# Batch 7 by block products too, with sums and softmax steps merged, and one pool of output tiles

## The chip, the core and the metric

The kernel runs on one core of a Trainium2 chip. The time is the device time of one execution in microseconds (us). TensorE (PE in the views; its weight loads are PEld) multiplies matrices into PSUM, which has eight banks of 512 fp32 columns here; VectorE (DVE) and ScalarE (ACT) read PSUM and SBUF; GpSimd (POOL) works from SBUF to SBUF and issues the loads; SyncE (SP) issues most stores. Each engine takes its instructions in order and waits on semaphores.

## What is computed

From the reference, for each of 8 batches b and 8 heads (576 tokens s, head size 64, 32 memory slots m):

```
a = exp(phi - max(phi));  a = a / sum(a)                 # over the 32 slots
k_m = a^T k;   v_m = a^T v                               # 32 x 64 per head
attn = softmax(scale * q @ k_m^T) @ v_m
x = attn, heads side by side                             # 4608 tokens x 512
h = max(x @ w1, x @ w2, x @ w3)                          # 4608 x 768
out = h @ w_out                                          # 4608 x 512, float32
```

## The kernel before

One function lays down every instruction; the order of the whole program is a list of words written out by hand at its end (manual schedule, line 55; the loop that reads the words ends the function). A word is a step, an index, "@" and a batch: `A1@3` is step A, index 1, batch 3 (batch 9 means the weights common to all batches). A "!" swaps the engine that a step uses by default. `issue` (L726) maps words to functions. An engine executes its instructions in the order of this list, each as soon as what it needs is there, so a step can run well before an earlier word of another engine. The PSUM banks that the steps take are a string of digits read off in the same order (L142).

The steps, by batch:

- Loads, all issued by POOL: L0 phi, L1 k, L2 v, L3 q (L85 to L112); r copies k beside v (L102; POOL, or ACT with "!").
- E: exp of phi (ACT). B: k_m and v_m (PE, L255). N: normalise (DVE). K: transposes (PE, L305) and their copy out of PSUM (L176 is the ACT branch of the common `evacuate`, L180 the DVE branch).
- Q0, Q1: q transposed in 32x32 blocks (DVE, L320). S: scores (PE, L340) and their exp (ACT, L349). Then the softmax over 32 slots, for each of two groups of heads by itself: a (DVE transpose, L394), s (DVE sum, L402), c (DVE reciprocal, L411), m (multiply, POOL L416, DVE with "!"), X (DVE transpose back, L424). Batch 0 and half of batch 1 do it another way (M, R, X with `ones_mul`).
- D0 to D3: v_m folded into the weights (PE L447, copied by ACT or DVE). So the product with the values needs only the softmax weights `attn` (256 rows) as input; V (DVE, L217, sources in SBUF) replaces w1 and w2 by their differences from w3, and the third term comes back as `wp3`, the fold of w3 times w_out.
- F0 to F11: the hidden layer, transposed (PE L473, four matmuls of 288 columns). Even steps write `h` (relu, ACT L174; DVE L178 with "!"); odd ones take the maximum with it into `hT` (DVE L486, one source in PSUM, one in SBUF).
- T0 to T4: an output tile of 128 tokens (PE, L662 six matmuls of hT and w_out, L671 two of attn and wp3, 512 columns each), copied by ACT or DVE and stored by SP. T4 is the tile of 128 tokens that spans the end of one batch and the start of the next; its attn part goes in two halves of 64 (L680). The last tile of all, T3@7, goes in two column halves (`ffn2_last`, L694: L703, L711) so that half is copied and stored while the other is computed.
- For batches 2 to 6 the 512 tokens outside T4 go by seven block products instead of eight (Strassen's scheme in Winograd's form): tokens, hidden rows and output columns are each cut in two. U0 to U3 form the sums of weight blocks (for batch 9 of w_out, for the others of wp3), A0 to A3 those of hT and A4 to A7 those of attn (`combine`, L509 to L511: POOL; DVE for U with "!" and for A without). P0 to P6 are the products (`products`, L569; PE L604: eight matmuls of 256 columns each), some of which add up in one bank, with copies taken of it in between (`snap`, `ln`, L618 or L616); sums and copies go into two fixed tiles `oj` (L645, L618, L616) that SP stores by block rows, 512 KB each (L649).

Batches 0, 1 and 7 go by token tiles: T0 to T3. `sums` (L525) puts the A sums of hT into space of w3 that is free by then, those of attn into `sa0`; hT and attn of two batches lie in two tiles.

Of the kernel before, what the change touches and what calls it, by code (L numbers as in the profile page):

```python
# [15 lines left out]
def kernel(  # L16
# [92 lines left out]
    def load_q(b):  # L109
        qq = inp.tile([P, NP, NC, D], BF16, name="qq", tag="qq")  # L110
        loaded.setdefault(b, {})["q"] = qq
        nc.gpsimd.dma_start(  # L112
            out=qq.rearrange("p j c d -> p j (c d)"), in_=by_pair(q, b)
        )
# [22 lines left out]
    for i in range(P // M):  # L137
# [7 lines left out]
            00232204420145545045024602460260426042672640640460246206420402640246240760260420  # L145
            64026402640264070462064026304620464060460624062403620460642640266042046204264260
            5620566620520652046262042062606262042640240630101323
# [177 lines left out]
    attns = {}  # L325

    def att_score(b):
# [4 lines left out]
        if b // 2 not in attns:  # L332
            attns[b // 2] = work.tile([P, NG, 2 * S], BF16, name="attn")
# [56 lines left out]

    def att_t(b, g):
        s = st[b]
        t = s["t", g] = work.tile([P, S // HP, R, 2], BF16, name="t", tag=f"t{g}")
        nc.vector.transpose(  # L394
            out=t.rearrange("p n r e -> p (n r e)").bitcast(FP32),
            in_=s["e2"][:, g].bitcast(FP32),
        )

    def att_sum(b, g):
        s = st[b]  # L400
        sm = s["sm", g] = work.tile([P, S // HP, 2], FP32, name="sm", tag=f"sm{g}")
        nc.vector.tensor_reduce(  # L402
            out=sm,
            in_=s["t", g].rearrange("p n r e -> p n e r"),
            op=ALU.add,
            axis=mybir.AxisListType.X,
        )

    def att_rec(b, g):
        s = st[b]  # L410
        nc.vector.reciprocal(out=s["sm", g], in_=s["sm", g])  # L411

    def att_mul(b, g, swap):
        s = st[b]
        t = s["t", g]
        (nc.vector if swap else nc.gpsimd).tensor_tensor(  # L416
            out=t,
            in0=t,
            in1=s["sm", g].unsqueeze(2).to_broadcast([P, S // HP, R, 2]),
            op=ALU.mult,  # L420
        )

    def att_back(b, g):
        nc.vector.transpose(  # L424
            out=attns[b // 2][:, g, (b % 2) * S : (b % 2 + 1) * S].bitcast(FP32),
            in_=st[b]["t", g].rearrange("p n r e -> p (n r e)").bitcast(FP32),
        )
# [32 lines left out]
    hts = {}  # L460
    fts = {}

    def ffn1(b, n, swap):
        s = st[b]
        ft, w = n // 2, n % 2
        if b // 2 not in hts:
            hts[b // 2] = work.tile([P, FT, 2 * S], BF16, name="hT")
# [16 lines left out]
        else:  # L484
            fts.setdefault(b, []).append(ft)
            nc.vector.tensor_tensor(  # L486
                out=hT[:, ft, (b % 2) * S : (b % 2 + 1) * S].rearrange("p (h n) -> p h n", h=2),
# [15 lines left out]
    sa0 = const.tile([P, 4, TW], BF16, name="sa0")  # L503
    oj0 = [const.tile([P, 2, DM], FP32, name=f"oj{i}") for i in range(2)]
# [20 lines left out]
    def sums(b):  # L525

        if b not in sas:
            if b == B - 1:
                s = inp.tile([P, NP, NC, D], BF16, name="sx", tag="qq")
                s = s.rearrange("p j c d -> p (j c d)").rearrange("p (i n) -> p i n", i=3)  # L530
                sa = inp.tile([P, NP, NC, D], BF16, name="sy", tag="qq")
                sa = sa.rearrange("p j c d -> p (j c d)")[:, 0 : 4 * TW]
                sa = sa.rearrange("p (i n) -> p i n", i=4)
            else:
                s, sa = w_sb[:, 0:3, 2], sa0
            sas[b] = (
                s.rearrange("p i (k q n) -> p i k q n", k=KT, q=2),
                sa.rearrange("p i (q n) -> p i q n", q=2),
            )
        return sas[b]  # L540

    def blocks(x, b, k):

        c0 = (b % 2) * (S + HP)
        x = x[:, :, c0 : c0 + 2 * TW]
        return [
            [
                x[:, k * i : k * (i + 1)].rearrange("p f (q r n) -> p f q r n", q=2, r=2)[
                    :, :, :, r
                ]  # L550
                for i in range(2)
            ]
            for r in range(2)
        ]

    def combine_a(b, i, on_dve):

        s, sa = sums(b)
        n = i % 4
        if i < 4:  # L560
            (a11, a12), (a21, a22) = blocks(hts[b // 2], b, KT)
            t = {0: s[:, 0], 1: s[:, 1], 2: a21, 3: s[:, 2]}
        else:
            (a11, a12), (a21, a22) = blocks(attns[b // 2], b, 1)
            t = {m: sa[:, m : m + 1] for m in range(4)}
        in0, in1 = [(a21, a22), (t[0], a11), (a11, a21), (a12, t[1])][n]
        combine(on_dve, t[n], in0, in1, ADD if n == 0 else SUB)

    def products(b, i, swap):  # L569

        s, sa = sums(b)
        h, a = blocks(hts[b // 2], b, KT), blocks(attns[b // 2], b, 1)
        wp3 = wp3s[b]

        def plain(r, c):
            return lambda k, q: h[r][c][:, k, q] if k < KT else a[r][c][:, 0, q]

        def summed(n):
            src = h[1][0] if n == 2 else s[:, min(n, 2)]
            return lambda k, q: src[:, k, q] if k < KT else sa[:, n, q]  # L580
# [43 lines left out]
        if "ot" not in acc:  # L624
            if b == B - 1:
                ot = [inp.tile([P, NP, NC, M], FP32, name=f"ox{n}", tag="ph") for n in range(2)]
                acc["ot"] = [
                    x.rearrange("p j c m -> p (j c m)")[:, 0 : 2 * DM].rearrange(
                        "p (q n) -> p q n", q=2
                    )  # L630
                    for x in ot
                ]
            else:
                acc["ot"] = oj0
        acc[i] = True
        done = [2] if i == 2 else [i] if i > 4 else [4] if 3 in acc and 4 in acc else []
        for n in done:
            ot = acc["ot"][n // 5][:, :, slice(0, CH) if n in (2, 6) else slice(CH, DM)]
# [7 lines left out]
            if n in (4, 6):  # L646
                r0 = b * S + (b % 2) * HP
                rows = out[r0 : r0 + 2 * TW].rearrange("(q r p) c -> p q r c", q=2, r=2)
                nc.sync.dma_start(out=rows[:, :, n // 5], in_=acc["ot"][n // 5])  # L649
# [3 lines left out]
    def ffn2(b, t, swap):  # L653
# [4 lines left out]
        if b == B - 1 and t == 3:  # L658
            return ffn2_last(b, c0)
        po = one_bank()  # L660
        for n, fc in enumerate(fts[b]):
            nc.tensor.matmul(  # L662
                po,
                lhsT=hT[:, fc, c0 : c0 + P],
# [23 lines left out]
        ot = opool.tile([P, DM], FP32, name="ot")  # L688
# [5 lines left out]
    def ffn2_last(b, c0):  # L694

        hT, attn = hts[b // 2], attns[b // 2]
        ot = opool.tile([P, DM], FP32, name="ot")
        r0 = (b // 2) * 2 * S + c0
        for i in range(2):
            c = slice(i * DM // 2, (i + 1) * DM // 2)  # L700
            po = one_bank()[:, 0 : DM // 2]
            for n, fc in enumerate(fts[b]):
                nc.tensor.matmul(  # L703
                    po,
                    lhsT=hT[:, fc, c0 : c0 + P],
                    rhs=wo_sb[:, fc, c],
                    start=(n == 0),
                    stop=False,
                )
            for g in range(NG):  # L710
                nc.tensor.matmul(  # L711
                    po,
                    lhsT=attn[:, g, c0 : c0 + P],
                    rhs=wp3s[b][:, g, c],
                    start=False,
                    stop=(g == NG - 1),
# [9 lines left out]
    def issue(b, n, swap):  # L726
# [6 lines left out]
            "L": lambda: load_ph(b) if i == 0 else load_q(b) if i == 3 else load_kv(b, i - 1),  # L733
            "H": lambda: load_kv(b, i % 2, halves[i // 2]),
# [27 lines left out]
    for w in """  # L762
# [3 lines left out]
        D2@0 D4@0 F4@0 L0@1 V1@0 F1@0 E@1 F3@0 L1@1 F5@0 F9@0 F7@0 L3@1 F11@0 L2@1 B0@1  # L766
        T2@0! N0@1 Q1@1 K0@1 L0@2 Q0@1 T1@0 S@1 U0@9 B1@1 U1@9 M1@1 U3@9! V2@0 N1@1 L1@2
        L2@2 K1@1! R1@1 L0@3 L3@2 a0@1 D0@1 L1@3 s0@1 D1@1! T0@0! r0@2 c0@1 m0@1! X0@1
        D2@1 X1@1 F6@1! F0@1 F10@1! F4@1! F1@1 F11@1 E@2 F8@1 F2@1 L2@3 F5@1 B@2 D3@1
        N@2 F3@1 L3@3 F7@1 K@2! F9@1 D3@2 L1@4 D0@2 L0@4 T3@0 Q1@2 U0@2 Q0@2 D2@2! S@2  # L770
        U1@2 a0@2 E@3 r0@3! s0@2 L2@4 L3@4 U2@9 c0@2 T3@1 T0@1! a1@2 m0@2 T4@1! D1@2!
        B@3 s1@2 c1@2 X0@2 m1@2 X1@2 F0@2 N@3 U3@2 Q0@3 A4@2! F6@2 A5@2! F1@2 U2@2 F8@2
        Q1@3 F2@2 L1@5 F7@2 L0@5 K@3! F4@2 F3@2 S@3 L2@5 A6@2! F5@2 A7@2! F10@2 a0@3
        D2@3 D0@3 D3@3 L3@5 a1@3 r0@4 s1@3 E@4 c1@3 s0@3 m1@3 c0@3 T1@1 F9@2 m0@3 F11@2
        T2@1! X0@3 D1@3! B@4 X1@3 N@4 F4@3 F6@3! F0@3 A0@2! F10@3 Q0@4 U0@3 Q1@4 A1@2!
        F8@3 F5@3 K@4! F9@3 U1@3 P1@2! S@4 A2@2! a0@4 A3@2! s0@4 D1@4! c0@4 L1@6 P0@2
        F11@3 P2@2 a1@4 s1@4 E@5 F7@3 P4@2 F2@3 c1@4 r0@5! F3@3 P5@2! F1@3 U3@3 L0@6
# [47 lines left out]
```

## Time and profile before

| | us |
|---|---|
| median of 3 runs (lowest, highest) | 163.0 (162.53, 163.24) |
| the profiled execution, whole | 162.93 |
| its span, first to last instruction | 161.2 |
| mean granted clock of TensorE | 0.997 |
| busy PE, DVE, ACT, POOL | 150.9, 113.0, 101.8, 103.8 |

The profile is of one execution. Its page gives the busy time of each engine, digits for 40 equal slices of the span, the chain of work that ended last, and the costliest groups of instructions (line, engine, operation, shapes, count; busy time and mean ns of one; idle time before them and what ended it). Other views of the same trace used below: the chain of waits in order of time, the timeline of a stretch, the table of stretches (busy time of each engine, granted clock, DMA share), and the DMA issues with the time from issue to landing.

### The profile page before, as it was taken

To read this page: it belongs to the slowest core of one execution; us is meant where nothing else is said; L and a number is where in the kernel's file an instruction comes from. 1 tells how busy PE (TensorE), PEld (TensorE's weight loads), DVE (VectorE), ACT (ScalarE), POOL (GpSimd) and SP (SyncE) were. 2 spreads that over 40 slices of the span, in tenths; PEclk is the share of its full clock that TensorE was granted. 3 is DMA by queue.
4 is the path that set the end of the run, shared out by engine and by line. 5 is a ranking of instruction groups with operands and counts; after the bars stand their busy time and mean duration, and the time that the engine had idled before them with its cause. 6 is when DMAs were issued, how large, how long until landed. Compare 5 with 4: busy or idle time off the path is not lost.

```text
span 161.2 us, 5135 instructions
## 1 busy us (share of the span) xinstructions
PE 150.9 (94%) x2190; PEld 98.5 (61%) x2202; DVE 113.0 (70%) x216; ACT 101.8 (63%) x144; POOL 103.8 (64%) x118
## 2 busy tenths in 40 slices
PE   7988698999899999899999999999999999999991
PEld 2343444673467346556788774887775878885660
DVE  2022702999878896697989799899889669785330
ACT  3205335943895798698598999977859864423110
POOL 7932135641056499979997999989959995840000
PEclk9999999999999999999999999999999999999998
DMA  5999999999999999999999999999304300601463
GB/s 154 188 204 191 194 210 212 279 207 276 251 277 259 208 228 229 338 225 223 317 213 240 211 331 230 176 230 268 133 32 168 132 4 0 260 0 40 162 255 133
DMA packets 21814, 31.78 MB, mean 197 GB/s; under 512 B 1056, under 2 KB 16416, under 8 KB 21792
## 3 DMA queue, kind: packets, MB, share of 16 engines
q0 software_dynamic: 16080, 21.43, 70.4%
q1 hardware_dynamic: 5568, 9.90, 17.2%
q8 instruction: 17, 0.28, 0.6%
q10 hardware_dynamic: 144, 0.13, 0.2%
q14 instruction: 5, 0.04, 0.1%
HBM read 39.32 MB, written 9.44 MB: 303 GB/s over the span
## 4 chain that ended last, share of the span: by engine, by line
PE 82%; DMA 9%; POOL 2%; ACT 2%; issue 2%; DVE 1%; ACTq 0%; DVEq 0%; POOLq 0%
PE psum L473 30%; PE psum L604 19%; PE psum L662 12%; DMA wo_sb<-in_moe_w_out_dram 9%; PE psum L447 5%; PE psum L196 3%; PE psum L671 3%; PE psum L255 3%; PE psum L340 2%; PE psum L680 1%; PE psum L305 1%; PE psum L703 1%; POOL ko L97 1%; ACT e L349 1%; DVE h L178 0%
## 5 line engine op out<-in xcount | busy, mean ns | idle before, releaser
L473 PE MATMUL psum<-attn,wp 128*128 128x288 bf16 x384 | 52.5, 286 | 0.2
L473 PEld LDWEIGHTS <-wp 128*128 128x128 bf16 x384 | 36.7, 98 | 11.0 <-issue 1.5
L486 DVE TENSOR_TENSOR hT<-psum,h 128x576 bf16<-128x576 f32 x48 | 34.5, 745 | 4.9 <-PE psum L473 3.2
L176 ACT CAST wp<-psum 128x1024 bf16<-128x1024 f32 (+1 forms) x30 | 28.4, 993 | 4.1 <-PE psum L447 2.8
L174 ACT ACTIVATE h<-psum 128x576 bf16<-128x576 f32 x36 | 22.3, 658 | 6.4 <-PE psum L473 6.2
L662 PE MATMUL psum<-wo_sb,hT 128*128 128x512 bf16 x81 | 21.0, 380 | 0.6 <-issue 0.2
L176 ACT COPY ot<-psum 128x512 f32<-128x512 f32 x14 | 8.1, 591 | 14.9 <-PE psum L671 8.1
L416 POOL TENSOR_TENSOR t<-t,sm 128x576 bf16<-128x576 bf16 x12 | 13.7, 1157 | 3.6 <-DVE sm L411 3.6
L662 PEld LDWEIGHTS <-hT 128*128 128x128 bf16 x90 | 8.2, 98 | 9.7 <-issue 1.7
L163 PE MATMUL psum<-warm 128*128 128x512 bf16 x42 | 12.5, 455 | 1.4 <-DVE warm L130 1.2
L604 PEld LDWEIGHTS <-hT 128*128 128x128 bf16 x120 | 11.5, 98 | 2.7 <-issue 0.9
L349 ACT ACTIVATE e<-psum 128x576 bf16<-128x576 f32 x16 | 9.5, 650 | 5.2 <-PE psum L340 5.1
L320 DVE STREAM_TRANSPOSE qT<-qq 128x576 f32<-128x576 f32 x16 | 11.7, 758 | 0.9 <-DMA qq<-in_q_dram 0.8
L178 DVE TENSOR_SCALAR h<-psum 128x576 bf16<-128x576 f32 x12 | 8.9, 752 | 3.5 <-PE psum L473 2.9
L511 POOL TENSOR_TENSOR w_sb<-hT 128x768 bf16<-128x768 bf16 x5 | 8.2, 1643 | 4.1 <-DVE hT L486 4.1
L233 ACT ACTIVATE e<-ph 128x1152 bf16<-128x1152 f32 (+1 forms) x9 | 9.7, 1073 | 1.9 <-DMA ph<-in_phi_dram 1.8
L645 DVE TENSOR_TENSOR oj<-psum,snap 128x512 f32<-128x512 f32 x10 | 6.8, 683 | 5.6 <-PE psum L604 3.9
L107 POOL COPY kvr<-ko 128x2304 bf16<-128x2304 bf16 x2 | 4.2, 2116 | 9.2 <-DMA ko<-in_k_dram 9.2
L604 PEld LDWEIGHTS <-w_sb 128*128 128x128 bf16 x90 | 8.6, 98 | 2.3 <-issue 0.7
L402 DVE TENSOR_REDUCE sm<-t 128x18 f32<-128x576 bf16 x13 | 9.5, 734 | 0.2
L447 PE MATMUL psum<-w_sb,kvt 64*32 64x512 bf16 (+1 forms) x200 | 9.3, 374 | 0.4 <-ACT kvt L176 0.4
L163 PEld LDWEIGHTS <-warm 128*128 128x128 bf16 x44 | 4.6, 113 | 7.5 <-issue 3.7
(97 smaller groups left out, 270.0 us busy)
## 6 DMA issues: line engine op xcount, KB each, us to landing
out_dram<-oj SPq DMA_DIRECT2D x10, 512.0 KB, 3.5
qq<-in_q_dram POOLq DMA_DIRECT2D x8, 576.0 KB, 16.4
ph<-in_phi_dram POOLq DMA_DIRECT2D x7, 576.0 KB, 17.4
ko<-in_k_dram POOLq DMA_DIRECT2D x7, 576.0 KB, 16.8
kvr<-in_v_dram POOLq DMA_DIRECT2D x7, 576.0 KB, 17.8
out_dram<-ot SPq DMA_DIRECT2D x15, 256.0 KB, 5.8
w_sb<-in_moe_w_dram POOLq DMA_DIRECT2D x3, 768.0 KB, 19.3
wo_sb<-in_moe_w_out_dram POOLq DMA_DIRECT2D x1, 768.0 KB, 14.9
```

The source lines that it names most:

```text
L163: nc.tensor.matmul(po[:, 0:BANK], lhsT=warm[:, 0:P], rhs=warm, start=True, stop=True)
L174: nc.scalar.activation(out=out_, in_=in_, func=AF.Relu)
L176: nc.scalar.copy(out=out_, in_=in_)
L233: nc.scalar.activation(out=s["e"][:, js], in_=loaded[b]["ph"][:, js], func=AF.Exp)
L320: nc.vector.transpose(out=s["qT"][:, j].rearrange("p j c r e -> p (j c r e)").bitcast(FP32), in_=loaded[b]["q"][:, j].rearrange("p j c d - ...
L349: nc.scalar.activation(out=e2[:, a].rearrange("p (t r c) -> p t r c", t=2, c=NC), in_=sc[a][:, :, 0:SH].rearrange("p t (c r) -> p t r c", ...
L416: (nc.vector if swap else nc.gpsimd).tensor_tensor(out=t, in0=t, in1=s["sm", g].unsqueeze(2).to_broadcast([P, S // HP, R, 2]), op=ALU.mult,)
L447: nc.tensor.matmul(ps[M * j : M * (j + 1), a, 0 : hi - lo], lhsT=lhs[r, M * j : M * (j + 1)], rhs=rhs[r, j, :], start=(i == 0), stop=(i == ...
L473: nc.tensor.matmul(acc[:, h, 0:SH], lhsT=wps[b][:, g, w * DF + ft * P : w * DF + (ft + 1) * P], rhs=attn[:, g, c0 : c0 + SH], start=(g == ...
L486: nc.vector.tensor_tensor(out=hT[:, ft, (b % 2) * S : (b % 2 + 1) * S].rearrange("p (h n) -> p h n", h=2), in0=a, in1=s["h1", ft], op=ALU.max,
L604: nc.tensor.matmul(po[:, q * CH : (q + 1) * CH], lhsT=lhs(k, q), rhs=rhs(k), start=(i < 3 and k == 0 and q == 0), stop=(k == KT and q == 1 ...
L662: nc.tensor.matmul(po, lhsT=hT[:, fc, c0 : c0 + P], rhs=wo_sb[:, fc, :], start=(n == 0), stop=False,)
```

## The change

Batch 7 gets steps A, U and P like batches 2 to 6; only T4 of batch 7 remains a token tile, and it now takes the path in two column halves, its attn matmuls first.

hT and attn share a tile `hx` of eight rows, three hidden rows and one attn group to each half, so that a sum of hT and the one of attn are one step: A0 to A3 of 1024 columns replace A0 to A3 of 768 and A4 to A7 of 256. For batch 7 the sums lie in two buffers that the q loads used.

The softmax steps a, s, c, m, X of batches 2 to 7 take both groups in one instruction.

Output tiles of T and P come from one pool of four tiles of 128 x 1024 (before: four of 128 x 512 for T, and the two fixed `oj`). In batch 7 each quarter is stored by itself.

The load of q for batch 1 is cut in two (J1, J0). The order of the list and the bank string are written anew from D2@0 on; before that they are as they were.

```diff
-    def load_q(b):
+    def load_q(b, h=slice(0, NP)):
...
         if b // 2 not in attns:
-            attns[b // 2] = work.tile([P, NG, 2 * S], BF16, name="attn")
+            x = hts[b // 2] = work.tile([P, FT + NG, 2 * S], BF16, name="hx")
+            attns[b // 2] = x.rearrange("p (i k) n -> p i k n", i=NG)[:, :, FT // NG]
...
     def att_t(b, g):
         s = st[b]
-        t = s["t", g] = work.tile([P, S // HP, R, 2], BF16, name="t", tag=f"t{g}")
+        if "t" not in s:
+            s["t"] = work.tile([P, NG, S // HP, R, 2], BF16, name="t", tag="t")
+        g = groups(g)
...
-    sa0 = const.tile([P, 4, TW], BF16, name="sa0")
-    oj0 = [const.tile([P, 2, DM], FP32, name=f"oj{i}") for i in range(2)]
...
-    def combine_a(b, i, on_dve):
-
-        s, sa = sums(b)
-        n = i % 4
-        if i < 4:
-            (a11, a12), (a21, a22) = blocks(hts[b // 2], b, KT)
-            t = {0: s[:, 0], 1: s[:, 1], 2: a21, 3: s[:, 2]}
-        else:
-            (a11, a12), (a21, a22) = blocks(attns[b // 2], b, 1)
-            t = {m: sa[:, m : m + 1] for m in range(4)}
+    def combine_a(b, n, on_dve):
+
+        s = sums(b)
+        (a11, a12), (a21, a22) = blocks(b)
+        t = [s[0], s[1], a21, s[2]]
         in0, in1 = [(a21, a22), (t[0], a11), (a11, a21), (a12, t[1])][n]
         combine(on_dve, t[n], in0, in1, ADD if n == 0 else SUB)
...
-            ot = acc["ot"][n // 5][:, :, slice(0, CH) if n in (2, 6) else slice(CH, DM)]
+            if ("ot", n // 5) not in acc:
+                acc["ot", n // 5] = opool.tile([P, 2, DM], FP32, name="ot")
+            ot = acc["ot", n // 5][:, :, slice(0, CH) if n in (2, 6) else slice(CH, DM)]
...
-        if b == B - 1 and t == 3:
+        if b == B - 1:
             return ffn2_last(b, c0)
```

Three places of the new list, as it has them (the swap of an A step with "!" is POOL, without it DVE):

```
... K0@1! Q0@1 T3@0 L2@2 Q1@1 S@1 L3@2 V2@0 U2@9 B1@1 L1@3 M1@1 V1@0 N1@1 a0@1 K1@1! ...
... F4@4! E@6 F8@4 F5@4 A0@3! F0@4 A1@3 U1@3! F10@4 U2@4 K@5 U0@4! L3@6 F2@4 P0@3 A3@3 U1@4! S@5
    F11@4 P1@3 D3@5 D0@5 a@5 s@5 P2@3 L0@7 A2@3! ...
... F5@6 F1@6 U1@6 F10@7 F0@7 A0@6 F6@7 A1@6 F2@7! F3@7 A3@6 F8@7 U1@7 P0@6 F5@7 F9@7 P1@6 F1@7 P2@6!
    F7@7 F11@7 U3@6 A0@7 P4@6 U3@7 A1@7 U2@6! P1@7 A2@6! P2@7! P3@6! U2@7! P5@6! P4@7 P0@7 P6@6 A3@7
    A2@7 P5@7! P3@7! P6@7! T4@7!
```

More of the change, by code (lines that the diff above doesn't have):

```diff
@@ L107, in pack @@
             nc.gpsimd.tensor_copy(out=out_, in_=in_)
-    def load_q(b):
-        qq = inp.tile([P, NP, NC, D], BF16, name="qq", tag="qq")
-        loaded.setdefault(b, {})["q"] = qq
+    def load_q(b, h=slice(0, NP)):
+        if "q" not in loaded.setdefault(b, {}):
+            loaded[b]["q"] = inp.tile([P, NP, NC, D], BF16, name="qq", tag="qq")
         nc.gpsimd.dma_start(
-            out=qq.rearrange("p j c d -> p j (c d)"), in_=by_pair(q, b)
+            out=loaded[b]["q"][:, h].rearrange("p j c d -> p j (c d)"),
+            in_=by_pair(q, b)[:, h],
         )
@@ L323, in att_q @@
         )
-    attns = {}
+    attns, hts = {}, {}
     def att_score(b):
@@ L389, in ones_mul, with groups @@
         )
+    def groups(g):
+        return slice(0, NG) if g is None else slice(g, g + 1)
     def att_t(b, g):
         s = st[b]
-        t = s["t", g] = work.tile([P, S // HP, R, 2], BF16, name="t", tag=f"t{g}")
+        if "t" not in s:
+            s["t"] = work.tile([P, NG, S // HP, R, 2], BF16, name="t", tag="t")
+        g = groups(g)
         nc.vector.transpose(
-            out=t.rearrange("p n r e -> p (n r e)").bitcast(FP32),
-            in_=s["e2"][:, g].bitcast(FP32),
+            out=s["t"][:, g].rearrange("p g n r e -> p (g n r e)").bitcast(FP32),
+            in_=s["e2"][:, g].rearrange("p g n -> p (g n)").bitcast(FP32),
         )
@@ L400, in att_sum @@
         s = st[b]
-        sm = s["sm", g] = work.tile([P, S // HP, 2], FP32, name="sm", tag=f"sm{g}")
+        if "ts" not in s:
+            s["ts"] = work.tile([P, NG, S // HP, 2], FP32, name="sm", tag="sm")
+        g = groups(g)
         nc.vector.tensor_reduce(
-            out=sm,
-            in_=s["t", g].rearrange("p n r e -> p n e r"),
+            out=s["ts"][:, g].rearrange("p g n e -> p (g n) e"),
+            in_=s["t"][:, g].rearrange("p g n r e -> p (g n) e r"),
             op=ALU.add,
@@ L409, in att_rec @@
     def att_rec(b, g):
-        s = st[b]
-        nc.vector.reciprocal(out=s["sm", g], in_=s["sm", g])
+        x = st[b]["ts"][:, groups(g)]
+        nc.vector.reciprocal(out=x, in_=x)
     def att_mul(b, g, swap):
         s = st[b]
-        t = s["t", g]
+        g = groups(g)
+        t = s["t"][:, g].rearrange("p g n r e -> p (g n) r e")
+        x = s["ts"][:, g].rearrange("p g n e -> p (g n) e").unsqueeze(2)
         (nc.vector if swap else nc.gpsimd).tensor_tensor(
@@ L423, in att_back @@
     def att_back(b, g):
+        g = groups(g)
+        out_ = attns[b // 2][:, g, (b % 2) * S : (b % 2 + 1) * S].bitcast(FP32)
         nc.vector.transpose(
-            out=attns[b // 2][:, g, (b % 2) * S : (b % 2 + 1) * S].bitcast(FP32),
-            in_=st[b]["t", g].rearrange("p n r e -> p (n r e)").bitcast(FP32),
+            out=out_, in_=st[b]["t"][:, g].rearrange("p g n r e -> p g (n r e)").bitcast(FP32)
         )
@@ L457, in fold, with row @@
         )
-    hts = {}
     fts = {}
+    def row(ft):
+        return ft + ft // (FT // NG)
     def ffn1(b, n, swap):
@@ L465, in ffn1 @@
         ft, w = n // 2, n % 2
-        if b // 2 not in hts:
-            hts[b // 2] = work.tile([P, FT, 2 * S], BF16, name="hT")
         hT, attn = hts[b // 2], attns[b // 2]
@@ L486, in ffn1 @@
             nc.vector.tensor_tensor(
-                out=hT[:, ft, (b % 2) * S : (b % 2 + 1) * S].rearrange("p (h n) -> p h n", h=2),
+                out=hT[:, row(ft), (b % 2) * S : (b % 2 + 1) * S].rearrange("p (h n) -> p h n", h=2),
                 in0=a,
@@ L569, in products @@
     def products(b, i, swap):
-        s, sa = sums(b)
-        h, a = blocks(hts[b // 2], b, KT), blocks(attns[b // 2], b, 1)
+        s, a = sums(b), blocks(b)
         wp3 = wp3s[b]
         def plain(r, c):
-            return lambda k, q: h[r][c][:, k, q] if k < KT else a[r][c][:, 0, q]
+            return lambda k, q: a[r][c][:, k, q]
         def summed(n):
-            src = h[1][0] if n == 2 else s[:, min(n, 2)]
-            return lambda k, q: src[:, k, q] if k < KT else sa[:, n, q]
+            src = a[1][0] if n == 2 else s[min(n, 2)]
+            return lambda k, q: src[:, k, q]
         def w_plain(i, j):
@@ L623, in products @@
             copy(t, x)
[L624 to L634, printed above, removed]
         acc[i] = True
@@ L645, in products @@
                 nc.vector.tensor_tensor(out=ot, in0=x, in1=y, op=ADD)
-            if n in (4, 6):
+            if n in (4, 6) or b == B - 1:
                 r0 = b * S + (b % 2) * HP
                 rows = out[r0 : r0 + 2 * TW].rearrange("(q r p) c -> p q r c", q=2, r=2)
-                nc.sync.dma_start(out=rows[:, :, n // 5], in_=acc["ot"][n // 5])
+                c = slice(0, DM) if b < B - 1 else slice(0, CH) if n in (2, 6) else slice(CH, DM)
+                nc.sync.dma_start(
+                    out=rows[:, :, n // 5, c], in_=acc["ot", n // 5][:, :, c]
+                )
     osts = {}
@@ L663, in ffn2 @@
                 po,
-                lhsT=hT[:, fc, c0 : c0 + P],
+                lhsT=hT[:, row(fc), c0 : c0 + P],
                 rhs=wo_sb[:, fc, :],
@@ L687, in ffn2 @@
                     )
-        ot = opool.tile([P, DM], FP32, name="ot")
+        ot = opool.tile([P, 2, DM], FP32, name="ot")[:, 0]
         r0 = (b // 2) * 2 * S + c0
@@ L696, in ffn2_last @@
         hT, attn = hts[b // 2], attns[b // 2]
-        ot = opool.tile([P, DM], FP32, name="ot")
+        ot = opool.tile([P, 2, DM], FP32, name="ot")[:, 0]
         r0 = (b // 2) * 2 * S + c0
-        for i in range(2):
-            c = slice(i * DM // 2, (i + 1) * DM // 2)
-            po = one_bank()[:, 0 : DM // 2]
+        cs = [slice(i * DM // 2, (i + 1) * DM // 2) for i in range(2)]
+        pos = [one_bank()[:, 0 : DM // 2] for _ in cs]
+        for c, po in zip(cs, pos):
+            for g in range(NG):
+                for u in range(2):
+                    nc.tensor.matmul(
+                        po[HP * u : HP * (u + 1)],
+                        lhsT=attn[:, g, c0 + HP * u : c0 + HP * (u + 1)],
+                        rhs=wp3s[b - 1 + u][:, g, c],
+                        start=(g == 0),
+                        stop=False,
+                        tile_position=(0, HP * u),
+                        skip_group_check=True,
+                    )
+        for i, (c, po) in enumerate(zip(cs, pos)):
             for n, fc in enumerate(fts[b]):
@@ L704, in ffn2_last @@
                     po,
-                    lhsT=hT[:, fc, c0 : c0 + P],
+                    lhsT=hT[:, row(fc), c0 : c0 + P],
                     rhs=wo_sb[:, fc, c],
[L707 to L714, printed above, removed]
                     start=False,
-                    stop=(g == NG - 1),
+                    stop=(n == FT - 1),
+                    skip_group_check=True,
                 )
@@ L733, in issue @@
             "L": lambda: load_ph(b) if i == 0 else load_q(b) if i == 3 else load_kv(b, i - 1),
+            "J": lambda: load_q(b, halves[i]),
             "H": lambda: load_kv(b, i % 2, halves[i // 2]),
@@ L792 @@
+        F11@7 U3@6 A0@7 P4@6 U3@7 A1@7 U2@6! P1@7 A2@6! P2@7! P3@6! U2@7! P5@6! P4@7
+        P0@7 P6@6 A3@7 A2@7 P5@7! P3@7! P6@7! T4@7!
     """.split():
```

85 lines of the change are left out of this document (34 added, 51 removed).

## The prediction

> **What bounds the kernel now.** I read the page first: busy times, then the chain that ended last.
>
> ```profile
> span 161.2 us, 5135 instructions
> ...
> PE 150.9 (94%) x2190; PEld 98.5 (61%) x2202; DVE 113.0 (70%) x216; ACT 101.8 (63%) x144; POOL 103.8 (64%) x118
> ...
> PE 82%; DMA 9%; POOL 2%; ACT 2%; issue 2%; DVE 1%; ACTq 0%; DVEq 0%; POOLq 0%
> ```
>
> TensorE is busy 94% of the span and makes 82% of the chain. A mean hides stages, so next the table of stretches (PE, PEld, DVE, ACT, POOL busy, then granted clock, DMA share, GB/s):
>
> ```profile
> 80.00:90.00 10.00, 10.00 (x199) 8.00 (x193) 9.40 (x21) 8.72 (x11) 8.77 (x9) 1.00 1.15 230
> ...
> 130.00:140.00 10.00, 10.00 (x98) 7.87 (x97) 8.67 (x14) 4.87 (x7) 7.38 (x8) 1.00 0.24 88
> ```
>
> From 70 to 155 us PE idles 0.36 us in all the stretches together: there time goes only if PE work goes, and a wait on PE is paid in full. DVE is the next engine, at 9.4 of 10. The profiled execution took 162.93 us, 1.73 around its span; the median is 163.0. I sum against 162.93.
>
> **PE work.** The prices are pieces of the chain of waits (start, us, what):
>
> ```profile
> 151.53 1.30 PE psum L662 x6
> 152.83 0.43 PE psum L671 x2
> 153.26 0.87 PE psum L604 x8
> ...
> 155.43 0.55 PE psum L680 x4
> 155.98 0.76 PE psum L703 x6
> 156.74 0.22 PE psum L711 x2
> 156.96 0.66 PE psum L703 x6
> 157.62 0.23 PE psum L711 x2
> ```
>
> A token tile costs 1.30 + 0.43 = 1.73, the split last one 1.87, a block product 0.87, T4 1.24 + 0.55 = 1.79. Removed: T0 to T2 of batch 7, 3 x 1.73 = 5.19, and T3, 1.87: 7.06. Added: 7 x 0.873 = 6.11. T4@7 in column halves: 12 matmuls at 0.109 (0.66/6) and the attn part in eight half-width ones, 0.55 as before: 1.87, so 0.08 more. Net **-0.87**. It is on the path: every one of these is PE work in the saturated stretch. The tail has the same form (half copied on ACT, stored from ACT), and costs the same.
>
> The Trainium skill (TensorE: Matmul & The Clock Gate, "Back-to-back issue gap") has a rule against this: a sustained stream gives about 81 ns per matmul at 128 columns and 131 at 512, so width is nearly free and halving it is dear. By an estimate on the line between them (98 ns at 256) seven products cost 5.5, the four tiles 4.7: 0.8 lost, 165.7 as the whole sum. The trace differs: 1.30/6 = 217 ns at 512 and 109 at 256. Both prices being rows of this kernel, I leave that outcome no chance.
>
> **Softmax and sums.** DVE per batch was 2 x (0.460 + 0.734 + 0.260 + 0.457) = 3.82. The merged transposes are of a size that the trace has (576 fp32: 0.758); the reduction of 1152 lies between 0.734 and twice that, 1.34 by the transposes' slope of 1.03 ns per element; reciprocal 0.28. So 3.14: six batches free 4.1 us on DVE. POOL's groups, and the same sum on DVE:
>
> ```profile
> L511 POOL TENSOR_TENSOR w_sb<-hT 128x768 bf16<-128x768 bf16 x5 | 8.2, 1643 | 4.1 <-DVE hT L486 4.1
> ...
> L511 DVE TENSOR_TENSOR hT<-hT 128x768 bf16<-128x768 bf16 x1 | 0.6, 550 | 0.0
> ```
>
> The group of 256 (`sa<-attn`) has 672 ns; with 1643 that is 1.9 ns per element: a merged sum of 1024 takes 2.13 on POOL instead of 2.31 for the pair; on DVE (550, and 280 at 256) 0.68. All this lies beside PE, which hardly waits there: between 0 and -0.36, taken as 0. The merged chain is about 0.5 us longer per batch (no group starts early); its tightest cover is batch 2, 7.2 us of PE work between S@2 and F2@2 (three T, four D, B@3) against 1.3 exp + 0.76 + 1.34 + 0.28 + 1.4 + 0.76 + hops = 6.3. Nothing, with 0.9 to spare; without cover 0.5 each.
>
> **Pool of tiles, loads, banks: nothing.** A store lands 3.5 to 5.8 us after issue, a pool of four turns over more slowly. The loads run at a DMA share over 1 and land one after another. The last (before: q of batch 7, issued 103.31, 11.5 to landing: 114.8) is now v, for B@7, which PE reaches at about 116: 1 us of cover, past that a wait of as much. Counting PE work between a bank's last matmul and its next use, 26 of 361 uses have under 0.9 us, against 28 of 362: same pressure.
>
> **V1 ahead of N1@1.** DVE now does V2 (row 39.42: 1.22) and V1 (row 31.30: 1.28) after Q1@1 (ends 39.07): to 41.6. N1@1, which K1@1 and D0@1 on PE wait for, ran at 41.19. U3@9's 0.52 has gone from there. **+0.3** (0 to 0.75).
>
> **Sums on DVE beside POOL: the disputed part.** Nine A sums go to DVE (before two, both after POOL's last). Before, one DVE instruction with two SBUF sources ran into a POOL sum (DVE timeline, then POOL):
>
> ```profile
> 28.72 1.67 DVE L217 TENSOR_TENSOR w_sb<-w_sb 128x2048 bf16<-128x2048 bf16 x1
> ...
> 39.42 1.22 DVE L217 TENSOR_TENSOR w_sb<-w_sb 128x2048 bf16<-128x2048 bf16 x1
> ```
>
> ```profile
> 27.68 1.63 POOL L511 TENSOR_TENSOR w3T<-wo_sb,w3T 128x768 bf16<-128x768 bf16 x1
> ```
>
> POOL was at work until 29.31, 0.59 into the first; it took 0.45 longer than its twin at 39.42. POOL's own spread is 1.632 to 1.657, so DVE work with one source in PSUM does not disturb it. I read it as DVE standing still until POOL ends.
>
> The Trainium skill (SBUF — State Buffer, "SBUF: two separate sides") says that a DVE operation with two SBUF inputs and a GpSimd operation exclude each other for a whole instruction. This row agrees; that it is the whole instruction no run here shows yet.
>
> Two places collide in the new order. First A1@3, U1@3 on DVE beside A2@3 on POOL. A0@3 starts when F7@3's maximum is there, then U2@4, two load issues, A2@3: 2.13 + 0.67 + 1.54 = 4.3 later, while PE goes from F7@3 to F5@4 through P6, T4, two D, B, P3, three F: 6.3, and DVE adds F5@4's maximum, 0.95 in all, before A1@3. F7@3's maximum is itself 1.5 late, so A2@3 starts 5.8 to 6.4 after F7@3's end, A1@3 wants to at 7.3, and A2@3 ends at about 8.2: a wait of 0.6 to 1.3, or of 2.1 (U1@3 then waits) if POOL is later than I think. K@5's copy is behind it on DVE, S@5 behind that on PE, with 0.16 to spare (2.51 of PE work against 2.35): 0.5 to 1.9 on PE, and I take the middle, **+1.2**. Second, A0@6 frees A1@6 on DVE and A2@6 on POOL at once. DVE reacts sooner (0.04 against 0.08 us in the softmax rows), so A2@6 runs after A1@6 and A3@6 waits 0.75 for it; the bank that F5@7 holds has 0.3 to spare: **+0.45** (0 to 1.6, if POOL gets in first).
>
> **Sum:** 162.93 - 0.87 + 0.3 + 1.2 + 0.45 = **164.0**.
>
> **Rivals.** *No exclusion, or it stays beside PE:* 162.93 - 0.87 + 0.3 = 162.4. For it: one row is thin evidence; against it, DVE is near PE's load there. Not slower. *The waits go as well:* 0.65 of "issue" at 66.99 and part of the wait at 40 to 42 need not come back; 161.7. Against it: DVE and POOL do not set PE's pace. *POOL first at both places* (slower by more): A1@6 then waits a whole sum, 1.6 instead of 0.45, and U1@3 2.1, PE 1.9 instead of 1.2: 165.9; it decides from the point where POOL's A2@3 is 0.8 us later than my sum.
>
> **How the numbers follow.** Forecast 164.0 (its own range 163.0 to 165.0): 50 in 100, of which 30 are over 163.8. No exclusion, 162.4: 30, of which 12 under 162.2. Waits go: 8. POOL first: 12. A measurement of this kernel tells about 0.5% (0.8 us) from no change. Faster 12 + 8 = 20, slower 30 + 12 = 42, the same 38. The range reaches from 162.0, leaving out the waits' case, to 165.4, leaving out POOL first: about 2 in 10 outside.
>
> **What would show it.** PE busy down by about 0.9. Sums on DVE of 128x1024 with a spread, 0.68 alone and above 1 beside POOL; an idle stretch on PE before S@5 and near F1@7, put down to DVE. Wrong: all nine at 0.68, or longer ones with PE still saturated. Merged transposes over 0.8 or a reduction over 1.5 would break the DVE sum; a DMA named as releaser of B@7 the loads'.

## The result, and the profile after

| | before | after |
|---|---|---|
| median of 6 runs (lowest, highest) | 162.97 (162.31, 163.24) | 163.84 (163.60, 164.14) |
| ratio (95% interval) | | 1.0063 (1.0040 to 1.0085) |
| the profiled execution, whole / its span | 162.93 / 161.2 | 164.14 / 162.4 |
| B1@0 on TensorE starts at (timeline) | 24.03 | 25.35 |
| from there to the end of the last matmul | 133.82 | 133.78 |
| of which TensorE busy / idle | 130.75 / 3.07 | 129.86 / 3.92 |

The forecast was 164.0. B1@0 is the last step on TensorE whose order the change leaves alone, so the last three rows separate the head (loads of the first weights) from what the change rewrites. The head was 1.3 us later in this one execution; the profiles of the ten experiments below, with the same order there, have it between 23.65 and 24.26 (one expectation below quotes 24.10 and 25.42 for these two, from the chain of waits, which sets this start 0.07 later). Behind B1@0 the two executions take the same time: 0.89 us less work, 0.85 more idling. Line numbers are now those of the changed kernel (F: PE L485, DVE maximum L498; A and U: L521; a, s, c, m, X: L401, L411, L420, L427, L437; P: L596; S: L342; V: L218).

The page of after, in the order read before (busy times, then the chain that ended last):

```profile
span 162.4 us, 5151 instructions
...
PE 151.7 (93%) x2218; PEld 102.1 (63%) x2228; DVE 119.8 (74%) x205; ACT 100.7 (62%) x143; POOL 95.7 (59%) x92
...
PE 76%; DMA 8%; DVE 5%; ACT 5%; issue 3%; POOL 1%; DVEq 0%; POOLq 0%
```

DVE went from 1% of the chain to 5%: the chain runs through DVE from 126.0 to 134.9 us. That is not yet a loss, since TensorE can be at work beside it. The table of stretches tells where (PE, PEld, DVE, ACT, POOL busy, granted clock, DMA share, GB/s):

```profile
90.00:100.00 10.00, 10.00 (x205) 7.65 (x190) 9.13 (x17) 9.34 (x14) 6.98 (x8) 1.00 1.12 269
...
130.00:140.00 10.00, 8.52 (x72) 6.78 (x71) 7.59 (x12) 3.50 (x7) 5.46 (x7) 1.00 0.28 107
140.00:150.00 10.00, 10.00 (x90) 8.52 (x88) 9.49 (x15) 4.71 (x8) 2.56 (x1) 1.00 0.01 2
```

The two places where the prediction saw DVE and POOL collide, at 94 and at 141 us, leave TensorE saturated. The loss stands at 130 to 140, a stretch that was full before, and it is one wait. The timelines of TensorE and of DVE there (start, length, engine, line; in brackets the idle time before and what ended it):

```profile
132.64 0.90 PE L485 MATMUL psum<-hx,wp 128*128 128x288 bf16 x6
134.93 0.90 PE L485 MATMUL psum<-hx,wp 128*128 128x288 bf16 x6 [1.40 <-DVE hx L437]
```

```profile
133.45 0.75 DVE L498 TENSOR_TENSOR hx<-psum,h 128x576 bf16<-128x576 f32 x1
134.11 0.77 DVE L437 STREAM_TRANSPOSE hx<-t 128x576 f32<-128x576 f32 x1
```

TensorE does F3@6 and two of the four matmuls of F0@6, stands 1.40 us until X@7 has ended, and goes on with the third. But F0@6 reads `attn` of batch 6, and X@7 writes `attn` of batch 7. The first step that needs X@7, F4@7, comes five steps later.

**The theory of the extent.** The merged X@7 writes rows 3 and 7 of `hx` (the two groups), columns of batch 7, in one instruction. Row 7, columns of batch 6, lies between its first and its last element. F0@6's first two matmuls read row 3 of batch 6, which lies ahead of the first element, and ran; its third reads row 7 and waited. So the waits of the program seem to be set by the stretch from the first element written to the last. **Rivals:** the merged softmax of batch 7 is late, and TensorE would stand at F4@7 anyway; or, the prediction's theory, the time is lost where DVE and POOL meet.

### The profile page after: what moved, and what is told of

Its sections match the earlier page's. It is cut to its first block, busy times and chain, and to the rows that moved or that the text cites. A ratio compares the mean times of both kernels' runs of the same rounds, so it can differ in the third digit from the quotient of the medians.

```text
span 162.4 us, 5151 instructions
## 1 busy us (share of the span) xinstructions
PE 151.7 (93%) x2218; PEld 102.1 (63%) x2228; DVE 119.8 (74%) x205; ACT 100.7 (62%) x143; POOL 95.7 (59%) x92
## 4 chain that ended last, share of the span: by engine, by line
PE 76%; DMA 8%; DVE 5%; ACT 5%; issue 3%; POOL 1%; DVEq 0%; POOLq 0%
PE psum L485 25%; PE psum L596 21%; PE psum L648 9%; DMA w_sb<-in_moe_w_dram 8%; PE psum L459 5%; PE psum L256 3%; PE psum L197 3%; PE psum L657 2%; ACT h L175 2%; PE psum L189 2%; PE psum L342 1%; DVE hx L498 1%; PE psum L666 1%; PE psum L164 1%; ACT wp L177 1%
## 5 line engine op out<-in xcount | busy, mean ns | idle before, releaser
L485 PE MATMUL psum<-hx,wp 128*128 128x288 bf16 x384 | 52.4, 286 | 1.9 <-DVE hx L437 1.4
L485 PEld LDWEIGHTS <-wp 128*128 128x128 bf16 x384 | 36.7, 98 | 13.3 <-issue 3.0
L498 DVE TENSOR_TENSOR hx<-psum,h 128x576 bf16<-128x576 f32 x48 | 34.2, 745 | 5.0 <-PE psum L485 2.9
L596 PEld LDWEIGHTS <-hx 128*128 128x128 bf16 x192 | 18.2, 98 | 3.6 <-issue 1.1
L648 PE MATMUL psum<-wo_sb,hx 128*128 128x512 bf16 x59 | 15.5, 380 | 0.5 <-issue 0.2
L427 POOL TENSOR_TENSOR t<-t,sm 128x1152 bf16<-128x1152 bf16 x5 | 10.6, 2129 | 4.3 <-DVE sm L420 3.5
L521 POOL TENSOR_TENSOR hx<-hx 128x1024 bf16<-128x1024 bf16 x5 | 11.1, 2218 | 3.6 <-DVE w_sb L521 3.5
L596 PEld LDWEIGHTS <-w_sb 128*128 128x128 bf16 x120 | 11.4, 98 | 2.5 <-issue 0.7
L112 POOL DMA_DIRECT2D qq<-in_q_dram x9 | 6.8, 757 | 8.0 <-DMA w_sb<-in_moe_w_dram 4.1
L648 PEld LDWEIGHTS <-hx 128*128 128x128 bf16 x66 | 6.0, 98 | 7.0 <-issue 1.3
L521 POOL TENSOR_TENSOR w_sb<-hx 128x1024 bf16<-128x1024 bf16 x4 | 8.5, 2128 | 2.9 <-DVE rden L276 2.3
L97 POOL DMA_DIRECT2D ko<-in_k_dram x9 | 7.0, 774 | 5.0 <-PE psum L256 2.1
L596 PE MATMUL psum<-wo_sb,hx 128*128 128x256 bf16 x72 | 9.9, 273 | 0.0
```

The source lines that it names most:

```text
L427: (nc.vector if swap else nc.gpsimd).tensor_tensor(out=t, in0=t, in1=x.to_broadcast(list(t.shape)), op=ALU.mult,)
L485: nc.tensor.matmul(acc[:, h, 0:SH], lhsT=wps[b][:, g, w * DF + ft * P : w * DF + (ft + 1) * P], rhs=attn[:, g, c0 : c0 + SH], start=(g == ...
L498: nc.vector.tensor_tensor(out=hT[:, row(ft), (b % 2) * S : (b % 2 + 1) * S].rearrange("p (h n) -> p h n", h=2), in0=a, in1=s["h1", ft], op ...
L521: eng.tensor_tensor(out=out_, in0=in0, in1=in1, op=op)
L596: nc.tensor.matmul(po[:, q * CH : (q + 1) * CH], lhsT=lhs(k, q), rhs=rhs(k), start=(i < 3 and k == 0 and q == 0), stop=(k == KT and q == 1 ...
L648: nc.tensor.matmul(po, lhsT=hT[:, row(fc), c0 : c0 + P], rhs=wo_sb[:, fc, :], start=(n == 0), stop=False,)
```

## Experiments

Each was timed against the kernel before on its own chip; ratios are to it. The changed kernel ran again beside three of them: the second run of the split X, U2@4 behind A2@3, and V1 early. Elsewhere a comparison with it goes by the ratios.

### Two X instead of one

```diff
-F3@6 X@7 F0@6
+F3@6 X0@7 X1@7 F0@6
```

> The step X of batch 7 in two instructions, one for each group of heads (X0@7, X1@7), all else as in the changed kernel. Theory of the extent: in the changed kernel F0@6 stood 1.40 us after two of its four matmuls, until X@7 was done, though it reads batch 6 and X@7 writes batch 7; the one X writes rows 3 and 7 of hx together, and row 7 of batch 6 lies between its first and its last element. With two instructions no element of batch 6 lies inside either. Then the 1.40 us of idle TensorE at 133.5 goes, F4@7 (the first true reader) comes some 2.6 us of TensorE work later and waits less than 0.3; DVE pays 0.15 more. Time 1.1 to 1.4 under the changed kernel: 162.4 to 162.8. Theory of the late chain (X@7 itself is too late and sets the end): the idle moves to F4@7, under 0.4 us is won: 163.5 to 163.9. Theory of the prediction (the two meetings of DVE and POOL cost 1.65): nothing changes, 163.8.

Measured: 161.63 (161.25 to 162.23), ratio 0.9900 (0.9869 to 0.9931). TensorE's and then DVE's timeline of the split X:

```profile
131.39 1.63 PE L485 MATMUL psum<-hx,wp 128*128 128x288 bf16 x12
132.86 0.82 PE L596 MATMUL psum<-w3T,hx 128*128 128x256 bf16 x6
```

```profile
132.87 0.83 DVE L437 STREAM_TRANSPOSE hx<-t 128x288 f32<-128x288 f32 x2
```

F3@6, F0@6 and F10@6 run as one block of 12 matmuls, and P6@5 follows while the two X are at work. F4@7 doesn't wait either: idle TensorE from 125 to 140 us is 0.09 in all. The compiled programs say the same: with one X the third matmul of F0@6 waits for X@7, with two the waits for them stand at F4@7. The theory of the extent holds, the late chain falls. The time came out lower than expected; the next group compares it with the changed kernel on one chip.

### The changed kernel and the split X side by side

> The changed kernel once more, unchanged, beside the others of this group. Its profiled execution reached B1@0 (the last step whose order the change leaves alone) at 25.42 us, against 24.10 in the kernel before and 23.65 to 23.88 in four variants of the changed kernel. Theory of the extent: that head of 25.42 was chance; it comes to 23.5 to 24.3 here, with 1.40 us of idle TensorE before F0@6, span 160.6 to 161.2, time 162.3 to 163.0, 1.2 to 1.5 above the split X. Rival: the later head belongs to the changed kernel (its tiles lie elsewhere), then B1@0 comes at 25 again and the time is 163.8.

> The split X of batch 7 (X0@7, X1@7) once more, to have it beside the changed kernel on one chip. Theory of the extent: 1.2 to 1.5 under the changed kernel, about 1.0% under the kernel before: 161.6. Rival (part of the first run's gain was the chip): 0.5 or less under the changed kernel.

Measured: the changed kernel 163.34 (162.88 to 163.83), ratio 1.0019 (0.9996 to 1.0043), B1@0 at 24.25, wait before the third matmul of F0@6 1.39; the split X 162.04 (161.34 to 162.64), ratio 0.9936 (0.9910 to 0.9962). So 1.30 us between them, as expected. The late head was not there. By its interval the first comparison gives a loss of 0.65 to 1.4 us, this one of -0.1 to 0.7. The split X is faster than the kernel before in both groups, by 1.0% and 0.6%, and than the changed kernel in the group that has it. Its profiled execution here, the slowest of its 12, has no wait at F0@6, but one of 1.83 for a load of v at 41.6 us.

### X@7 one place later in the list

```diff
-F3@6 X@7 F0@6
+F3@6 F0@6 X@7
```

> The word X@7 goes one place back, behind F0@6, which issues nothing on DVE: the order on every engine stays as in the changed kernel, and only what F0@6 waits for changes. X@7 stays one instruction, and runs as late as before. Theory of the extent: F0@6 runs through, and F10@6, now the first matmul step behind X@7, stands after its second matmul instead; TensorE does 0.49 us (one F step) more before the wait: idle 1.40 becomes about 0.9, time 0.5 under the changed kernel: 163.3. Theory of the late chain: X@7 ends at the same moment, the work behind it takes as long, and only what was done ahead of it counts; if F4@7 were what stands, nothing is won: 163.8. Theory of the prediction: 163.8.

Measured: 162.98, ratio 0.9977 (0.9957 to 0.9998). TensorE's timeline of it:

```profile
131.82 1.39 PE L485 MATMUL psum<-hx,wp 128*128 128x288 bf16 x10
134.11 0.41 PE L485 MATMUL psum<-hx,wp 128*128 128x288 bf16 x2 [0.90 <-DVE hx L437]
```

Ten matmuls (F3@6, F0@6 and half of F10@6) instead of six, then the wait, 0.90 instead of 1.40: the difference is one F step, 0.49. No engine's order was changed. What waits is the first reader of row 7 that stands behind X@7 in the list, whichever it is.

### The same merge in the kernel before

In the kernel before, X1@7 and X0@7 become one instruction; the `t` tiles of the two groups are laid side by side for it. In the compiled program this changes TensorE's waits at one place: the third matmul of F7@6 now waits for DVE, and three waits for DVE shortly behind it, which it covers, are gone.

```diff
-        t = s["t", g] = work.tile([P, S // HP, R, 2], BF16, name="t", tag=f"t{g}")
+        if "t" not in s:
+            s["t"] = work.tile([P, NG, S // HP, R, 2], BF16, name="t", tag="t")
+        t = s["t", g] = s["t"][:, g]
...
-m1@7 X1@7 X0@7 A3@5!
+m1@7 X@7 A3@5!
```

> The kernel before, with one thing of the change: the transposes back of batch 7, X1@7 and X0@7, become one instruction for both groups (the t tiles of the two groups lie in one tile for that, for all batches). a, s, c, m and all else stay as they are. Theory of the extent: in the kernel before, F7@6 follows X@7 in the list and reads attn of batch 6, whose second group lies between the two rows that the one X writes. F7@6 then stands after two of its four matmuls until X@7 is done. In the profile of before, F7@6's third matmul ran at about 133.8 and the two X ended at 134.79: TensorE stands 0.8 to 1.1 us there, and the time is 0.6% above the kernel before: 163.9. Rival (the wait of the changed kernel comes from its merged chain being late, not from the one X): nothing changes, as DVE does the same work, 0.06 us less: 163.0.

Measured: 164.98 (164.22 to 165.47), ratio 1.0107 (1.0072 to 1.0143). In the kernel before, F7@6 ran in one block with its neighbours:

```profile
133.09 1.63 PE L473 MATMUL psum<-attn,wp 128*128 128x288 bf16 x12
```

With one X, TensorE's, then DVE's timeline (here F is L481, X L427):

```profile
133.53 0.41 PE L481 MATMUL psum<-attn,wp 128*128 128x288 bf16 x2
135.21 1.39 PE L481 MATMUL psum<-attn,wp 128*128 128x288 bf16 x10 [1.28 <-DVE attn L427]
```

```profile
134.39 0.77 DVE L427 STREAM_TRANSPOSE attn<-t 128x576 f32<-128x576 f32 x1
```

Two matmuls, a wait of 1.28 until X has ended, then the third: the wait of the changed kernel, brought into the other one by this edit alone. It is a little longer than my 0.8 to 1.1: in the kernel before the block begins at 133.09, so F7@6's third matmul ran at about 133.3 and not at 133.8. The time rose by 1.2 to 2.3, more than the 0.9 that I wrote. This profile has another 0.95 on a load of weights at 31 us, as three profiles of the changed order have it (0.44, 0.69 and 1.04); whether all six runs had it is not shown. Taken out of the one kernel and put into the other, the one X of batch 7 is shown to make this wait. That the rule behind it is the stretch from first to last element fits which matmul stood in all of them, and that with two X none did. It fits the elements too: a row of `hx` has 1152, so X@7 writes 4032 to 4607 and 8640 to 9215, and the third matmul of F0@6 reads 8064 to 8351, none of them written by X@7. No run looks at the rule itself.

### A shorter queue ahead of the chain

```diff
-D2@6 D0@7! P4@5
+D2@6 D0@7 P4@5
```

> The copy of D0@7 (1.18 us on DVE at 127.31, just ahead of the transpose a@7) goes to ACT, which has idle time there. X@7 keeps its one instruction and its place. Theory of the extent: what costs is the distance from the end of X@7 to F0@6; a@7, s@7, c@7, m@7 start about 1.1 earlier, X@7 then waits for the maximum of F3@6 ahead of it on DVE, and ends 0.7 to 1.1 earlier: idle TensorE at 133.5 falls from 1.4 to 0.3 to 0.7, less what ACT's later copies (relu of F8@6, F6@6) cost, 0 to 0.5: 162.8 to 163.5. Theory of the prediction (meetings of DVE and POOL): no change, 163.8.

Measured: 164.54, ratio 1.0076 (1.0048 to 1.0103): my own expectation missed. DVE's, then TensorE's timeline:

```profile
133.59 0.75 DVE L498 TENSOR_TENSOR hx<-psum,h 128x576 bf16<-128x576 f32 x1
134.26 0.77 DVE L437 STREAM_TRANSPOSE hx<-t 128x576 f32<-128x576 f32 x1
```

```profile
135.08 0.90 PE L485 MATMUL psum<-hx,wp 128*128 128x288 bf16 x6 [1.40 <-DVE hx L437]
```

m@7 ended at 132.1 here instead of 133.2, and yet the wait is the same 1.40. X@7 stands behind the maximum of F3@6 on DVE, which can't start before F3@6 is done. So the wait is a round trip, TensorE to the maximum (0.75) to X (0.77) and back, less the two matmuls of F0@6. In these two kernels it doesn't depend on how early the softmax chain is: X@7 began 0.9 us after m@7's end in the one, 2.1 in the other. What ACT's later copies cost shows as two more waits on TensorE, 0.18 and 0.40.

### The meetings of DVE and POOL

```diff
-F10@4 U2@4 K@5
+F10@4 U2@4 U2@4 K@5
```

> The weight sum U2@4 on POOL is computed twice, so that A2@3 behind it on POOL starts 0.6 us later and meets A1@3 on DVE nearer to its start. In the changed kernel A1@3 (at 94.29) met the last 0.64 us of A2@3 and took 1.21 us, not 0.69; K@5's copy behind it on DVE ended at 95.96 and S@5 on TensorE began at 96.03, without a wait. Theory of the prediction's exclusion, with no cover left: A1@3 takes 1.8 us, K@5's copy comes 0.6 later, TensorE stands 0.5 to 0.65 before S@5: 164.3 to 164.5. Rival, exclusion with cover: A1@3 is longer but TensorE stands under 0.2: 163.9. Rival, no exclusion (the 1.21 us has another cause): A1@3 stays at 1.2 or goes back to 0.7, and TensorE does not stand: 163.8.

```diff
-F10@4 U2@4 K@5
+F10@4 K@5
...
-L0@7 A2@3!
+L0@7 A2@3! U2@4
```

> The changed kernel (X@7 in one) with U2@4 behind A2@3 on POOL, so that A2@3 ends 0.6 us earlier and A1@3 on DVE no longer meets it. Exclusion with the cover as the trace shows it (S@5 began 0.07 us behind K@5's copy, without a wait): A1@3 takes 0.7 us instead of 1.2, and TensorE gains nothing: as the changed kernel. Theory of the prediction (the meeting costs 1.2 on TensorE): 1.0 or more under the changed kernel.

First the meeting as the changed kernel has it: DVE (A1@3, U1@3, K@5's copy), POOL (A2@3), and the chain of waits (P0@3, S@5).

```profile
94.29 1.21 DVE L521 TENSOR_TENSOR w_sb<-w_sb,hx 128x1024 bf16<-128x1024 bf16 x1
95.42 0.28 DVE L521 TENSOR_TENSOR twb<-wp,twb 128x256 bf16<-128x256 bf16 x1
95.62 0.34 DVE L181 COPY kvt<-psum 128x384 bf16<-128x384 bf16 x1
```

```profile
92.79 2.14 POOL L521 TENSOR_TENSOR hx<-hx 128x1024 bf16<-128x1024 bf16 x1
```

```profile
95.16 0.87 PE psum L596 x8
96.03 0.47 PE psum L342 x22
```

POOL's sum ends at 94.93; A1@3, 0.69 when alone, ends 0.57 later. The copy ends at 95.96 and S@5 follows P0@3 at 96.03 without a gap. With U2@4 twice (DVE, POOL, TensorE):

```profile
93.10 2.30 DVE L521 TENSOR_TENSOR w_sb<-w_sb,hx 128x1024 bf16<-128x1024 bf16 x1
```

```profile
92.69 2.14 POOL L521 TENSOR_TENSOR hx<-hx 128x1024 bf16<-128x1024 bf16 x1
```

```profile
95.92 0.48 PE L342 MATMUL psum<-qT,kvt 32*32 32x288 bf16 x32 [1.08 <-DVE kvt L181]
```

Measured: 164.49, ratio 1.0080 (1.0050 to 1.0111). A2@3 moved by 1.09 against A1@3 (0.74 for the second sum, 0.28 of idling before the load issue behind it), A1@3 grew by as much, and TensorE stands 1.08 us: exclusion, and with the cover used up it costs TensorE one for one. The shift was larger than planned, so the time is at the upper end of what I wrote.

With U2@4 behind A2@3: 163.64, ratio 1.0039 (1.0013 to 1.0064), 0.30 above the changed kernel of its group: no gain. The meeting is gone, and a new one is there (DVE's A1@3 and U1@3, then POOL's U2@4):

```profile
93.47 0.68 DVE L521 TENSOR_TENSOR w_sb<-w_sb,hx 128x1024 bf16<-128x1024 bf16 x1
94.07 0.76 DVE L521 TENSOR_TENSOR twb<-wp,twb 128x256 bf16<-128x256 bf16 x1
```

```profile
93.46 1.22 POOL L521 TENSOR_TENSOR twb<-wp 128x256 bf16<-128x256 bf16 x1
```

A1@3 takes 0.68; U2@4 on POOL, 0.67 alone, stands for it; and U1@3, 0.28 alone, stands for U2@4. By the trace U2@4 begins 0.01 ahead of A1@3 and yet A1@3 goes through first, so starts as close as this don't tell the order.

### V ahead of N1@1

Both on the split X:

```diff
-F3@0 F4@0 F9@0
+F3@0 F4@0 V1@0 F9@0
...
-M1@1 V1@0 N1@1
+M1@1 N1@1
```

> The split X, and besides V1@0 goes back ahead of the maximum of F9@0 on DVE, as early as the kernel before has it, so that N1@1 has only V2@0 in front of it. Theory of the prediction (V1 ahead of N1@1 costs TensorE 0.3): 0.3 under the split X alone: 161.3, with N1@1 0.7 earlier and K1@1 on TensorE 0.3 earlier. Rival, from the trace of the changed kernel: N1@1 ended at 42.42 and K1@1, which needs it, ran only at 42.95, behind M1@1, which stood 0.67 us for an exp of S@1 on ACT, late behind the copy of T3@0; then nothing changes, 161.6.

```diff
-M1@1 V1@0 N1@1 a0@1
+M1@1 N1@1 V1@0 a0@1
```

> The split X, and V1@0 goes behind N1@1 on DVE (just ahead of a0@1), so that N1@1 has only V2@0 in front of it and runs 1.2 us earlier, if B1@1 is there. Theory of the prediction (V1 ahead of N1@1 costs TensorE 0.3): K1@1 comes 0.3 earlier against S@1, time 0.3 under the split X (161.3 to 161.7). Rival, from the traces of the changed kernel: K1@1 is behind M1@1 on TensorE, and M1@1 and B1@1 wait for ACT's exp and for a load of v; N1@1 is ready in time either way: nothing changes, K1@1 stays as far behind S@1 as in the split X.

Measured: V1 early 163.13, ratio 0.9991 (0.9965 to 1.0017), 1.1 slower than the split X of its group; V1 behind 162.68, ratio 0.9971 (0.9948 to 0.9993), no gain (the split X, not in this group, had 0.9900 and 0.9936). Of V1 early, TensorE's, DVE's and POOL's timeline; then DVE's of V1 behind:

```profile
37.49 0.80 PE L256 MATMUL psum<-ko,e 64*32 64x128 bf16 x72 [1.32 <-DVE hx L498]
```

```profile
34.60 2.17 DVE L218 TENSOR_TENSOR w_sb<-w_sb 128x1024 bf16<-128x1024 bf16 x2
```

```profile
33.95 1.66 POOL L521 TENSOR_TENSOR w3T<-wo_sb 128x768 bf16<-128x768 bf16 x1
```

```profile
42.31 0.29 DVE L280 TENSOR_TENSOR kvn<-psum,rden 128x128 bf16<-128x128 f32 x1 [1.15 <-PE psum L256]
```

Put early, V1 runs into U0@9 on POOL (its two halves take 2.17, alone 1.28), the maxima behind it are late, and TensorE stands 1.32 for a bank. Put behind, N1@1 has nothing in front of it and waits 1.15 for B1@1. K1@1 comes 2.08 after S@1, as in the changed kernel run again (39.77 and 41.85) and in the kernel before (39.47 and 41.55). V1 ahead of N1@1 costs nothing. The time of V1 behind does not decide this by itself, since V1 now holds up a0@1 and the steps after it: TensorE waits 0.58 and 0.24 for DVE at 46 to 47 us, which the split X does not.

## Why the prediction was right in the number and wrong in its parts

- **PE work, -0.87: right.** TensorE's busy time behind B1@0 fell by 0.89, and by 0.75 and 0.89 in the repeated changed kernel and the first run of the split X (130.00 and 129.86 against 130.75). The Trainium skill (TensorE: Matmul & The Clock Gate, "Back-to-back issue gap") would, by the estimate made from it, have had 0.8 added; the trace disagrees with it here too.
- **Prices of the merged forms: right but for one.** Transposes 0.76, reduction 1.35, sums of 1024 2.13 on POOL and 0.69 on DVE; the reciprocal took 0.37, not 0.28.
- **Pool of tiles, loads, banks, nothing: right.** Between 45 us and the end of the last matmul the first profile has no idle stretch of TensorE over 0.1 us but the 1.40, so none of the three held it there.
- **"The merged chain ... Nothing, with 0.9 to spare": the step that failed.** I weighed only the length of the chain, and batch 2 as its tightest place. What the merge costs is a wait: one X over two groups holds up steps of the neighbouring batch that read between them. 1.40 us, all on TensorE.
- **A1@3 beside A2@3, +1.2: mechanism right, place and cover wrong.** A1@3 met the last 0.64 us of A2@3 and lost 0.52, below my 0.6 to 1.3; and the copy had some 0.5 to spare, not 0.16, since without that loss it would have ended at 95.44 for an S@5 at 96.03. TensorE lost nothing. The experiment with U2@4 twice shows how near it was.
- **A3@6, +0.45: DVE first, as said, cost nothing.** A3@6 took 1.08, so 0.40 longer, not 0.75, and TensorE has 10.00 of 10 there. The sign that I named, an idle stretch before S@5 and near F1@7, is absent.
- **V1 ahead of N1@1, +0.3: not there.** M1@1 did wait 0.67, for the exp of S@1, late on ACT behind T3@0's copy. But the kernel before waits 0.41 at B1@1 and 0.20 at M1@1, and K1@1 is no further behind S@1 in the one than in the other; both experiments leave N1@1 out of it.
- **"The waits go as well": partly.** The 0.65 of issue inside S@3 is in before and, as 0.59, in its variant with one X, and in no profile of the changed order. Something is left of it there: S@3 takes 0.67 in the first profile where S@1 takes 0.47, and three other profiles have 0.17 to 0.36 of issue shortly behind S@3. What it comes from is open.

So 1.95 us of forecast costs were mostly not there, and a wait of 1.40 that I had not seen stood in for them: that the number came out is luck. The rival "it stays beside PE" tells what the two meetings did, and its 162.4 is near the split X (161.63 and 162.04), which has no such wait. Behind B1@0: -0.89 + 1.40 - 0.65, and 0.10 from smaller waits, comes to -0.04. The repeated changed kernel has 133.97 there, 0.15 more than before, and 0.31 more in its time. The 0.87 of the first comparison is more than these; its profile has the rest in the head, and why all six of its runs came out so high stays open. The mean granted clock was 0.989 in two of the six and 0.997 or more in the others, so the clock alone doesn't tell it.

## What to carry to other kernels

When two instructions are merged into one that writes two separate rows, look at what lies between the rows: steps behind it in the list that read there can wait for it, whatever they need. The waits of the compiled program name such a step before anything runs. In a trace, a wait is read from the matmul at which it stands and not only from the step: that two of four had run told which operand was held. And a forecast that hits as a sum has to be looked at stage by stage; each term has its own stretch of the profile.

## What the runs showed of the hardware

The sums of DVE with two sources in SBUF and those of POOL took turns here, in both directions. In the changed kernel A1@6 on DVE began 0.11 ahead of A2@6 on POOL, and A3@6 ran into its end (DVE, then POOL):

```profile
140.95 0.69 DVE L521 TENSOR_TENSOR w_sb<-w_sb,hx 128x1024 bf16<-128x1024 bf16 x1
...
143.09 1.08 DVE L521 TENSOR_TENSOR w_sb<-hx,w_sb 128x1024 bf16<-128x1024 bf16 x1
```

```profile
141.06 2.56 POOL L521 TENSOR_TENSOR hx<-hx 128x1024 bf16<-128x1024 bf16 x1 [3.54 <-DVE w_sb L521]
```

POOL lost 0.43 of the 0.58 that A1@6 still had to run; A3@6 ended 0.55 after POOL. In the three meetings with an A sum on POOL (0.52, 0.40 and 1.61 lost by DVE, of 0.64, 0.53 and 1.73 side by side) the DVE sum ends 0.55 to 0.57 after POOL's, a little less than its own length alone. That is what the Trainium skill (SBUF — State Buffer, "SBUF: two separate sides") says, whoever starts first holds the port for the whole instruction; these runs agree, up to the 0.12 to 0.15 by which each loss is shorter than the time side by side.

In the first profile of the changed kernel the granted clock was 0.86 between 10 and 20 us (0.50 from 18 to 20), and the 24 transposes of w3 took 2.72 us instead of 1.51, after a wait of 1.19 for the load. In before, a wait of 1.48 that ended three microseconds later left the clock at 1.00. What lowered it is open.
